# A planner's durations, a conversion cut into single steps and a broadcast matmul operand, in an attention and two-MLP kernel

## Chip, cores and metric

One NeuronCore of one Trainium2 chip runs the whole kernel in one launch. The metric is the device time of a run in microseconds. Engines are called as in the profile: PE is TensorE (PEld its weight loads), DVE is VectorE, ACT is ScalarE, POOL is GpSimd, SP is SyncE, whose queue issues every DMA of this kernel.

## What is computed

Inputs are q, k, v of 8 batches, 8 heads, 576 positions and 64 features, and five weight matrices. The weights come as float64 (the reference scales a float32 array with a numpy double), q, k, v as float32.

```python
q_s = softmax(q over the 64 features);  k_s = softmax(k over the 576 positions)
kv = einsum('bhsd,bhse->bhde', k_s, v);  x = einsum('bhsd,bhde->bhse', q_s, kv)   # 4608 x 512
h = x @ w_in;  x = relu(h)**2 @ w_out                      # w_in 512 x 2048
x = (sigmoid(x @ w_gate) * (x @ w_val)) @ w_out2           # w_gate, w_val 512 x 1536
```

## The kernel before, in words

**Work.** The 4608 tokens are cut into nine blocks `j` of 512; heads go in four pairs `p`. For each batch `b` and pair, `plan_k` (lines 604 to 621) loads keys and values and forms the 128x128 `kv`; for each block and pair, `plan_q` (623 to 659) makes the softmax of the queries and multiplies it with `kv` into `x`. [...] Blocks 0 to 2 go through the first MLP by plain products (`c_in`, `c_out`, lines 809 to 839); the other blocks, and all of the second MLP, go through units of seven products instead of eight (`plan_seven`, 768).

**Weights.** A raw weight block is 128x512 float64 (512 KB) in a buffer `wraw` of tag "W". Its conversion to float32 is done with integer operations: two on ACT (`w_abs` line 255, `w_low` line 261), then on DVE `w_bits`, which issues three instructions one behind the other on the same tile (a clip, line 268; a shift and mask, 269; the sign, 272), and `w_round` (line 279). Then the block is split (212, 215) and stored to a DRAM copy (`w_store`, line 297, or `w_store32`, line 310); later products fetch the copy (`w_fetch`, line 302). There are 68 raw blocks, 32 of them for the first MLP.

**Keys' maxima.** The maximum of each key feature over all positions is needed in all 128 partitions. `k_max` (411) takes maxima within a partition, `k_turn` (423) transposes on PE into PSUM, `k_diag` (428 to 434) reduces along the row to one value per partition, `m1` (line 431), and multiplies the identity matrix with it (line 433); `k_all` (436 to 438) multiplies a matrix of ones (stationary operand) with that diagonal (moving operand), which puts each maximum into all rows. `k_sub` (443) and `k_exp` (447) follow, then the product with the values (`k_mm`, 453) and its scaling (`k_rec` 457 and 458, `k_copy` 465).

**The order.** Nothing is left to a scheduler of the compiler: the class `Plan` (30 to 131) writes the order of every queue. Each step is added with a key (a due time, computed from constants such as T0 = 27.0 and TS0 = 4.4), the engines that it may use with its assumed duration in us, the steps it comes after, and the buffers it takes and gives. `Plan.trace` plays this list through: when an engine is idle in the plan, the ready step with the smallest key is issued to it, occupies it for the assumed duration, and its successors become ready after `LATENCY` more (2.0 us behind a DMA, 0.2 behind PE, 0.15 behind the others). A pair as a duration stands for "POOL idle, POOL busy"; no step is planned on POOL in this kernel, so the first value always counts (lines 103, 104). The plan's clock is used for the order alone. On the chip every queue runs in that order, and an instruction waits by semaphore for what it needs, with all that stands behind it in its queue. The assumed durations of the steps around the change are: DVE on a 128x512 tile 0.78 (`TT`, 199), `w_bits` 1.55, `w_round` 0.85, ACT on such a tile 0.60 to 0.66, `k_diag` 0.5, `k_mm` 1.3, a 512 KB DMA 1.5, a load of q 0.73. Steps of q and k of blocks above 4 are offered to PE 2.5 us late (`SLACK`, 601); those of blocks up to 4 are not.

Of the kernel before, what the change touches and what calls it, by code (L numbers as in the profile page):

```python
# [29 lines left out]
class Plan:  # L30
# [4 lines left out]
    LATENCY = {DMA: 2.0, PE: 0.2}  # L35
# [19 lines left out]
    def trace(self):  # L55
# [22 lines left out]
        while left:  # L78
            for e in ready:
                if busy[e] > now:  # L80
                    continue
                held = []
                short = set()
                while ready[e] and len(held) < self.LOOK:
                    key, n = heapq.heappop(ready[e])
                    if taken[n]:
                        continue
                    _, _, engines, name, fn, args, _, take, give, _ = self.ops[n]
                    if any(t in short for t in take) or any(self.free[t] < take.count(t) for t in take):
# [12 lines left out]
                    us = engines[e]  # L102
                    if isinstance(us, tuple):
                        us = us[busy[POOL] > now]
# [41 lines left out]
def attention_mlp_mlp(  # L146
# [44 lines left out]
    ones = cst.tile([128, 128], F32, name="ones")  # L191
# [7 lines left out]
    TT = (0.78, 1.1)  # L199
    VEC = {DVE: TT}  # L200
    LOW = {DVE: TT}
    ROUND = {DVE: 0.85}
# [208 lines left out]
    def k_max(b, p):  # L411
# [9 lines left out]
        kmx[b, p] = (a, mx[:, C:2 * C])  # L421

    def k_turn(b, p):
        ps = banks[p] if b == 0 else pa.tile([128, N], F32, tag="pa", name="kps")
        nc.tensor.transpose(ps[:, KT0:KT0 + 128], kmx[b, p][0], ident)
        kps[b, p] = ps

    def k_diag(b, p):
# [175 lines left out]
    def plan_k(b, p, key, step, wait=()):  # L604
# [5 lines left out]
        add(key, {DVE: (0.95, 1.9)}, ("kmx",) + n, k_max, b, p, after=[("kt",) + n], take=["km"])  # L610
        add(key + 0.5 * step, {PE: 0.3}, ("kt2",) + n, k_turn, b, p, after=[("kmx",) + n], take=bank, slack=slack(b))
        add(key + step, {DVE: (0.5, 0.85)}, ("kdg",) + n, k_diag, b, p, after=[("kt2",) + n])
        add(key + 1.5 * step, {PE: 0.4}, ("kgm",) + n, k_all, b, p, after=[("kdg",) + n], give=["km"], slack=slack(b))
        add(key + 2 * step, {DVE: 0.85}, ("ks",) + n, k_sub, b, p, after=[("kgm",) + n])
        add(key + 3 * step, {ACT: 0.75}, ("ke",) + n, k_exp, b, p, after=[("ks",) + n])
        add(key + 4 * step, {PE: 1.3}, ("kp",) + n, k_mm, b, p, after=[("ke",) + n, ("vt",) + n], give=big, slack=slack(b))
        add(key + 5 * step, {DVE: 0.4}, ("kr",) + n, k_rec, b, p, after=[("kp",) + n], take=["kr"])
# [5 lines left out]
    def plan_q(j, p, key, step, qmul):  # L623
# [3 lines left out]
        add(key, {DVE: 0.69}, ("qa",) + n, q_red, j, p, ALU.max, "qm", after=[("qt",) + n], take=["qm"])  # L627
# [4 lines left out]
        else:  # L632
            add(key + 0.5 * step, {DVE: (0.8, 0.9) if pe else (0.95, 1.2)}, ("qs",) + n, q_sub, j, p, after=[("qa" if pe else "qaw",) + n], give=["qm"] if pe else ["qm", "pa"])
        add(key + step, {ACT: 2.4 if j == JACT else 0.63}, ("qe",) + n, q_exp, j, p, after=[("qs",) + n], give=["qm"] if j == JACT else [])
        add(key + 2 * step, {DVE: 0.69}, ("qb",) + n, q_red, j, p, ALU.add, "qr", after=[("qe",) + n], take=["qr"])
        if not pe:
            add(key + 2.3 * step, {PE: 0.15}, ("qbw",) + n, q_swap, j, p, after=[("qb",) + n], take=["pa"], slack=slack(j))
        add(key + 2.5 * step, {DVE: (0.3, 0.6) if pe else (0.45, 0.9)}, ("qr",) + n, q_sum, j, p, after=[("qb" if pe else "qbw",) + n], give=[] if pe else ["pa"])
        if j == JACT:
            qmul = {ACT: 2.4}  # L640
# [127 lines left out]
    def plan_seven(uid, t, nb, n, pe, tags):  # L768
# [8 lines left out]
        ua = 0.6 if n > 256 else 0.35  # L777
        uv = 0.7 if n > 256 else 0.42
# [153 lines left out]
    def conv_in(j, f, t):  # L932
# [20 lines left out]
        add(t + 2.6, {ACT: 1.24}, ("cg", j, f), c_g, j, f, after=[("ch", j, f, KT - 1)], take=["f"])  # L953

    def conv_out(j, f, t):
# [7 lines left out]
        add(t - 2.5, {ACT: 0.62}, ("chi", j, f), c_hi, j, f, after=[("cg", j, f)], take=["S"])  # L963
# [91 lines left out]
    def in_stage(n, t):  # L1055
# [5 lines left out]
        for h in range(2):  # L1061
            G = ("G", n, h)
            gready = defaultdict(dict)
            for u in range(2):
# [12 lines left out]
            for kk in range(4):  # L1077
                for qn, (name, where) in gready[kk].items():
# [7 lines left out]
                    add(tk, {ACT: 0.63}, ("bhi", nm, qn), lambda nm=nm, qn=qn, bind=bind: (bind(), b_hi(nm, qn, qn, "S", nt)), after=[name], take=["S"])  # L1086
# [5 lines left out]
            for tq in range(2):  # L1092
# [16 lines left out]
                for oh in range(2):  # L1109
                    pr = use_pair[tq, oh]  # L1110
                    ends = []
                    for m in range(2):
# [7 lines left out]
                        add(t + 0.1, {DVE: 0.7} if h else {ACT: 0.6, DVE: 0.7}, nm, o_ev, key, pr[m], h, nt, CHOSEN, after=after, take=[] if h else ["a"])  # L1120
# [7 lines left out]
    def gate_stage(n, t):  # L1128
# [10 lines left out]
        for u in range(gv_n):  # L1139
# [5 lines left out]
            us = 0.62 if nt > 256 else 0.38  # L1145
            uv = 0.7 if nt > 256 else 0.42
# [83 lines left out]
    nc.gpsimd.memset(ones, 1.0)  # L1230
# [68 lines left out]
```

## Time and profile before

| what | value |
|---|---|
| median of 3 runs | 1712.14 us (1710.82 to 1718.0) |
| the profiled execution's own time | 1716.33 us |
| span of the profile (first to last instruction) | 1714.5 us |
| mean granted PE clock | 0.990 of full speed |
| instructions | 24259 |

The profile is of one execution. The span lies inside the execution's time; what lies around it is 1.8 us. A matmul's end in the trace is modelled, and matmuls overlap, so that a busy PE is one that always has a matmul in flight. In a timeline a line is: start, duration, engine, line of the kernel, operation, output and inputs, count, and in brackets how long the engine was idle before it and what ended that idle time.

### The profile page before, as it was taken

Reading aid. Unit: us, or ns where it says so; the run is one execution under the profiler, and the core shown is the slowest. Engines: PE = TensorE matmul, PEld = TensorE weight load, DVE = VectorE, ACT = ScalarE, POOL = GpSimd, SP = SyncE. Lnnn points to the kernel's source line nnn. Section 1 sums busy time; section 2 is a strip of 40 time slices with the busy share of each in tenths; the row PEclk is TensorE's granted clock in tenths of the full one; section 3 lists DMA queues with packets and bytes.
Section 4 is the critical chain, followed back from the end, with each engine's and each line's share of the span. In section 5 each row is a group of like instructions: output and inputs, shape, how many; then the busy total and the mean of one; then the engine's idle time right before and its main releaser. Section 6 shows DMA issues by size and latency. Waiting matters only on the chain.

```text
span 1714.5 us, 24259 instructions
## 1 busy us (share of the span) xinstructions
PE 1666.9 (97%) x8788; PEld 1425.3 (83%) x8788; DVE 1127.2 (66%) x2109; ACT 916.4 (53%) x1649; POOL 2.1 (0%) x15
## 2 busy tenths in 40 slices
PE   5889999999999999999999999999999999999999
PEld 3668878787788788878898889988888899889999
DVE  7978746788888665775785757741624485448556
ACT  4986544557576565653554655552723454335344
POOL 0000000000000000000000000000000000000000
PEclk8989999999999999999999999999999999999999
DMA  6999878799787889799757555755576557655797
GB/s 228 335 329 325 312 241 289 250 324 368 255 309 267 321 293 349 270 370 335 246 185 243 190 188 172 237 201 183 186 249 194 195 190 246 204 196 178 245 378 270
DMA packets 149144, 443.23 MB, mean 259 GB/s; under 512 B 15648, under 2 KB 24864, under 8 KB 149024
## 3 DMA queue, kind: packets, MB, share of 16 engines
q1 hardware_dynamic: 149024, 441.68, 74.1%
q8 instruction: 70, 1.15, 0.3%
q14 instruction: 50, 0.41, 0.1%
HBM read 354.06 MB, written 87.56 MB: 258 GB/s over the span
## 4 chain that ended last, share of the span: by engine, by line
PE 85%; DMA 7%; DVE 4%; ACT 2%; issue 1%; SPq 1%; ACTq 0%; DVEq 0%
PE bank L218 27%; PE bank L220 27%; PE bank L219 27%; PE xps L580 2%; PE kps L453 1%; DMA qt<-in_q_dram 1%; DMA ws<-w_in 1%; DMA wraw<-in_moe_w_gate_dram 1%; DMA wraw<-in_moe_w_out_dram 1%; DMA vt<-in_v_dram 1%; DMA ws<-w_gv 1%; DVE whl L215 0%; PE qsw L511 0%; PE bank L453 0%; ACT wf L255 0%
## 5 line engine op out<-in xcount | busy, mean ns | idle before, releaser
L218 PE MATMUL bank<-bX,ws 128*128 128x512 f32 (+1 forms) x1176 | 446.3, 379 | 7.2 <-DMA ws<-w_in 5.7
L220 PE MATMUL bank<-bX,ws 128*128 128x512 f32 (+1 forms) x1176 | 440.7, 375 | 0.0
L219 PE MATMUL bank<-bX,ws 128*128 128x512 f32 (+1 forms) x1176 | 440.7, 375 | 0.0
L739 DVE TENSOR_TENSOR s<-s,bank 128x512 f32<-128x512 f32 (+1 forms) x279 | 179.9, 651 | 215.4 <-PE bank L220 178.4
L212 ACT ACTIVATE s<-bank 128x512 f32<-128x512 f32 (+1 forms) x279 | 156.7, 568 | 215.4 <-PE bank L220 213.7
L218 PEld LDWEIGHTS bank<-bX,ws 128*128 128x128 f32 x1176 | 222.0, 189 | 47.5 <-DMA ws<-w_in 4.7
L220 PEld LDWEIGHTS bank<-bX,ws 128*128 128x128 f32 x1176 | 221.7, 189 | 40.3
L219 PEld LDWEIGHTS bank<-bX,ws 128*128 128x128 f32 x1176 | 222.1, 189 | 37.7 <-issue 0.5
L212 ACT ACTIVATE bS<-s 128x512 fp32r<-128x512 f32 (+1 forms) x282 | 166.1, 597 | 147.1 <-PE bank L220 129.7
L215 DVE TENSOR_TENSOR bS<-s,bS 128x512 fp32r<-128x512 f32 (+1 forms) x282 | 180.9, 650 | 75.2 <-ACT bS L212 67.7
L218 PE MATMUL bank<-ws,bS 128*128 128x256 f32 x756 | 214.6, 284 | 0.0
L220 PE MATMUL bank<-ws,bS 128*128 128x256 f32 x756 | 213.9, 283 | 0.0
L219 PE MATMUL bank<-ws,bS 128*128 128x256 f32 x756 | 213.9, 283 | 0.0
L218 PE MATMUL bank<-bS,ws 128*128 128x512 f32 x384 | 150.5, 392 | 0.0
L220 PE MATMUL bank<-bS,ws 128*128 128x512 f32 x384 | 149.5, 389 | 0.0
L219 PE MATMUL bank<-bS,ws 128*128 128x512 f32 x384 | 149.5, 389 | 0.0
L218 PEld LDWEIGHTS bank<-ws,bS 128*128 128x128 f32 x756 | 145.0, 192 | 1.0 <-issue 0.2
L219 PEld LDWEIGHTS bank<-ws,bS 128*128 128x128 f32 x756 | 145.0, 192 | 0.9 <-issue 0.2
L220 PEld LDWEIGHTS bank<-ws,bS 128*128 128x128 f32 x756 | 145.0, 192 | 0.0
L758 ACT ACTIVATE s<-s 128x512 f32<-128x512 f32 (+1 forms) x120 | 70.4, 588 | 136.4 <-DVE s L739 136.2
L212 ACT ACTIVATE whl<-wf 128x512 fp32r<-128x512 f32 x111 | 68.0, 624 | 42.2 <-PE bank L220 12.0
L215 DVE TENSOR_TENSOR whl<-wf,whl 128x512 fp32r<-128x512 f32 x111 | 74.1, 685 | 20.3 <-ACT whl L212 19.3
(122 smaller groups left out, 2419.8 us busy)
## 6 DMA issues: line engine op xcount, KB each, us to landing
ws<-w_gv SPq DMA_DIRECT2D x210, 512.0 KB, 4.3
ws<-w_out SPq DMA_DIRECT2D x185, 512.0 KB, 4.3
ws<-w_in SPq DMA_DIRECT2D x116, 512.0 KB, 6.0
w_gv<-whl SPq DMA_DIRECT2D x42, 512.0 KB, 5.7
w_out<-whl SPq DMA_DIRECT2D x37, 512.0 KB, 6.2
w_in<-whl SPq DMA_DIRECT2D x32, 512.0 KB, 4.4
wraw<-in_moe_w_out_dram SPq DMA_DIRECT2D x28, 512.0 KB, 6.1
vt<-in_v_dram SPq DMA_DIRECT2D x32, 325.0 KB, 5.9
```

The lines of the kernel that those rows point to most:

```text
L212: nc.scalar.activation(out=dst, in_=src, func=AF.Copy)
L215: by_name[engine].tensor_tensor(out=dst, in0=src, in1=hi.bitcast(F32), op=ALU.subtract)
L218: nc.tensor.matmul(ps, ah, bh, start=first, stop=False, skip_group_check=True)
L219: nc.tensor.matmul(ps, ah, bl, start=False, stop=False, skip_group_check=True)
L220: nc.tensor.matmul(ps, al, bh, start=False, stop=last, skip_group_check=True)
L453: nc.tensor.matmul(ps[:, 0:2 * D + 1], kt[:, r, :], vt[:, r, 0:2 * D + 1], start=(r == 0), stop=(r == RK - 1))
L580: nc.tensor.matmul(ps[:, e], kvf[b % 2][p], t[:, e], start=True, stop=True)
L739: nc.vector.tensor_tensor(out=t, in0=t, in1=banks[pr[b]][:, 0:n], op=ALU.add)
L758: nc.scalar.activation(out=t, in_=t, func=AF.Sigmoid)
```

## The change

Three edits.

1. **Keys' maxima.** `k_diag` loses the multiplication with the identity and becomes `k_col`; `k_all` takes `m1`, a 128x1 tile, as stationary operand read 128 times (`to_broadcast`), and the identity as the moving one. The tile of ones and its memset go.
2. **Conversion.** `w_bits` is planned as three steps, `w_clip`, `w_bits` and `w_sign`, of one instruction each, with keys 0.05 apart. The instructions are the same.
3. **The planner's durations.** Pairs are gone; almost every duration on DVE and ACT, and some on PE, are other numbers, and `LATENCY` gets entries for DVE and ACT. Durations of DMAs, the due times, the buffers and `SLACK` stay.

The diff, cut to its core:

```diff
-    LATENCY = {DMA: 2.0, PE: 0.2}
+    LATENCY = {DMA: 2.0, PE: 0.2, DVE: 0.13, ACT: 0.15}
...
-    TT = (0.78, 1.1)
+    TT = 0.61
...
-    ROUND = {DVE: 0.85}
+    ROUND = {DVE: TT}
+    AS, AP = 0.53, 0.5
...
+    def w_clip(key):
+        t = wf[key]
+        nc.vector.tensor_scalar(out=t, in0=t, scalar1=E_MIN, scalar2=E_MAX, op0=ALU.max, op1=ALU.min)
+
     def w_bits(key):
-        _, high = w_words(key)
         t = wf[key]
         w = t.bitcast(I32)
-        nc.vector.tensor_scalar(out=t, in0=t, scalar1=E_MIN, scalar2=E_MAX, op0=ALU.max, op1=ALU.min)
         nc.vector.tensor_scalar(
             out=w, in0=w, scalar1=3, scalar2=0x3FFFFFF8, op0=ALU.logical_shift_left, op1=ALU.bitwise_and
         )
+
+    def w_sign(key):
+        _, high = w_words(key)
+        w = wf[key].bitcast(I32)
         nc.vector.scalar_tensor_tensor(
             out=w, in0=high, scalar=-0x40000000, in1=w, op0=ALU.bitwise_and, op1=ALU.bitwise_or
         )
...
-        add(t, {ACT: 0.63}, ("wh",) + key, w_hi, key, b, htag, after=after, take=[htag])
+        add(t, {ACT: AS}, ("wh",) + key, w_hi, key, b, htag, after=after, take=[htag])
...
-            add(t, {ACT: 0.66}, ("wa",) + key, w_abs, key, tag, after=[("wl",) + key])
-            add(t + 0.1, {ACT: 0.66}, ("wc",) + key, w_low, key, after=[("wl",) + key])
-            add(t + 0.2, {DVE: (1.55, 2.05)}, ("wb",) + key, w_bits, key, after=[("wa",) + key])
-            add(t + 0.4, ROUND, ("wr",) + key, w_round, key, CHOSEN, after=[("wb",) + key, ("wc",) + key], give=["W"])
+            add(t, {ACT: 0.57}, ("wa",) + key, w_abs, key, tag, after=[("wl",) + key])
+            add(t + 0.1, {ACT: 0.57}, ("wc",) + key, w_low, key, after=[("wl",) + key])
+            add(t + 0.2, {DVE: 0.35}, ("wp",) + key, w_clip, key, after=[("wa",) + key])
+            add(t + 0.25, {DVE: 0.35}, ("wb",) + key, w_bits, key, after=[("wp",) + key])
+            add(t + 0.3, {DVE: TT}, ("wg",) + key, w_sign, key, after=[("wb",) + key])
+            add(t + 0.4, ROUND, ("wr",) + key, w_round, key, CHOSEN, after=[("wg",) + key, ("wc",) + key], give=["W"])
...
-    def k_diag(b, p):
+    def k_col(b, p):
         m1 = sp.tile([128, 1], F32, tag="km1", name="km1")
         nc.vector.tensor_reduce(out=m1, in_=kps[b, p][:, KT0:KT0 + 128], axis=AX.X, op=ALU.max)
-        _, dg = kmx.pop((b, p))
-        nc.vector.tensor_scalar(out=dg, in0=ident, scalar1=m1, scalar2=None, op0=ALU.mult)
-        kmx[b, p] = dg
+        kmx[b, p] = m1
 
     def k_all(b, p):
-        nc.tensor.matmul(kps[b, p][:, KM0:KM0 + 2 * D], ones, kmx.pop((b, p)), start=True, stop=True)
+        m1 = kmx.pop((b, p)).to_broadcast([128, 128])
+        nc.tensor.matmul(kps[b, p][:, KM0:KM0 + 2 * D], m1, ident, start=True, stop=True)
...
-        add(key + step, {DVE: (0.5, 0.85)}, ("kdg",) + n, k_diag, b, p, after=[("kt2",) + n])
+        add(key + step, {DVE: 0.22}, ("kdg",) + n, k_col, b, p, after=[("kt2",) + n])
...
-        add(key + 4 * step, {PE: 1.3}, ("kp",) + n, k_mm, b, p, after=[("ke",) + n, ("vt",) + n], give=big, slack=slack(b))
+        add(key + 4 * step, {PE: 1.15}, ("kp",) + n, k_mm, b, p, after=[("ke",) + n, ("vt",) + n], give=big, slack=slack(b))
...
-        add(key + step, {ACT: 2.4 if j == JACT else 0.63}, ("qe",) + n, q_exp, j, p, after=[("qs",) + n], give=["qm"] if j == JACT else [])
+        add(key + step, {ACT: 2.1 if j == JACT else AS}, ("qe",) + n, q_exp, j, p, after=[("qs",) + n], give=["qm"] if j == JACT else [])
...
-        ua = 0.6 if n > 256 else 0.35
-        uv = 0.7 if n > 256 else 0.42
+        ua = AP if n > 256 else 0.28
+        uv = TT if n > 256 else 0.34
...
```

The lines that are left out put `AS` (0.53) for 0.62 to 0.63 and `AP` (0.5) for 0.6 on ACT, `TT` (0.61) for 0.69 to 0.85 on DVE, 1.12 for 1.24 in the two-instruction steps on ACT, and small cuts of the same kind elsewhere.

## Rows read from the trace of the kernel before

**Rows 1.** The page: busy us of each engine, share of the span, instructions.
```profile
PE 1666.9 (97%) x8788; PEld 1425.3 (83%) x8788; DVE 1127.2 (66%) x2109; ACT 916.4 (53%) x1649; POOL 2.1 (0%) x15
```

**Rows 2.** Busy time by stretch: stretch, length, PE, PEld, DVE, ACT, POOL, clock, DMA share, GB/s.
```profile
0.00:20.00 20.00, 8.58 (x38) 6.53 (x39) 13.89 (x38) 8.67 (x16) 2.10 (x15) 1.00 0.82 297
20.00:40.00 20.00, 12.58 (x41) 8.13 (x40) 15.93 (x37) 10.96 (x21) 0.00 (x0) 0.64 0.38 144
40.00:120.00 80.00, 69.20 (x300) 51.82 (x299) 66.48 (x147) 69.53 (x165) 0.00 (x0) 0.92 0.94 333
120.00:860.00 740.00, 725.78 (x3352) 600.19 (x3352) 542.13 (x1036) 431.88 (x763) 0.00 (x0) 1.00 0.84 301
860.00:1715.00 855.00, 850.76 (x5064) 758.62 (x5062) 488.73 (x854) 395.34 (x687) 0.00 (x0) 1.00 0.65 216
```

**Rows 3.** DVE's timeline from 20 to 45 us.
```profile
22.45 0.42 DVE L268 TENSOR_SCALAR wf<-wf 128x512 f32<-128x512 f32 x1
22.90 0.43 DVE L269 TENSOR_SCALAR wf<-wf 128x512 int32<-128x512 int32 x1
23.36 0.69 DVE L272 SCALAR_TENSOR_TENSOR wf<-wraw,wf 128x512 int32<-128x512 int32 x1
24.95 0.16 DVE L457 TENSOR_SCALAR kri<-bank 128x1 f32<-128x1 f32 x1 [0.90 <-PE bank L453]
...
26.27 0.29 DVE L431 TENSOR_REDUCE km<-bank 128x1 f32<-128x128 f32 x1 [0.38 <-PE bank L425]
26.60 0.29 DVE L433 TENSOR_SCALAR kmx<-ident,km 128x128 f32<-128x128 f32 x1
...
32.72 0.69 DVE L215 TENSOR_TENSOR x<-xps,x 128x512 fp32r<-128x512 f32 x1 [0.91 <-ACT x L212]
34.24 0.16 DVE L457 TENSOR_SCALAR kri<-bank 128x1 f32<-128x1 f32 x1 [0.83 <-PE bank L453]
...
34.82 0.64 DVE L279 CUSTOM_DVE_ANT_0 wf<-wraw,wf 128x1024 uint16<-128x1024 uint16 x1
35.37 0.69 DVE L557 TENSOR_TENSOR qt<-qt,qst 128x512 f32<-128x512 f32 x1
35.97 0.69 DVE L279 CUSTOM_DVE_ANT_0 wf<-wraw,wf 128x1024 uint16<-128x1024 uint16 x1
```

**Rows 4.** The SP queue's timeline, the two issues between 23 and 36 us.
```profile
29.29 0.33 SPq L489 DMA_DIRECT2D qt<-in_q_dram  x1
35.48 0.33 SPq L310 DMA_DIRECT2D w_in<-wf  x1
```

**Rows 5.** The chain of waits in order of time: one values product early, one later.
```profile
22.40 2.52 PE bank L453 x10
...
226.27 1.11 PE kps L453 x10
```

**Rows 6.** PE's waits from 120 us on: line, releaser, us in total, times, longest.
```profile
PE bank L218 <- DMA ws<-w_in: 5.7, 4, 2.9
PE qsw L511 <- DVE qst L501: 3.0, 2, 1.9
PE bank L218 <- DMA ws<-w_gv: 1.5, 1, 1.5
```

**Rows 7.** Groups by line and form: busy us and mean ns of one, idle time before.
```profile
L438 PEld LDWEIGHTS kps<-kmx,ones 128*128 128x128 f32 x56 | 10.1, 188 | 3.8 <-DVE kmx L433 2.0
L511 PEld LDWEIGHTS qsw<-qst,swap 128*128 128x128 f32 x112 | 19.3, 189 | 12.8 <-DVE qst L501 3.8 <-DVE x L215 2.8 <-ACT xf L212 1.5
L433 DVE TENSOR_SCALAR kmx<-ident,km 128x128 f32<-128x128 f32 x32 | 9.2, 287 | 1.1
L535 ACT ACT_TABLE_LOAD x9 | 11.5, 1283 | 5.5 <-DMA qt<-in_q_dram 4.4 <-DVE qt L526 1.0
```

**Rows 8.** DMA issues: kind, count, KB each, median us from issue to landing.
```profile
ws<-w_in SPq DMA_DIRECT2D x116, 512.0 KB, 6.0
...
qt<-in_q_dram SPq DMA_DIRECT2D x36, 256.0 KB, 4.5
```

More of the change, by code (lines that the diff above doesn't have):

```diff
@@ L102, in trace @@
                     us = engines[e]
-                    if isinstance(us, tuple):
-                        us = us[busy[POOL] > now]
                     busy[e] = now + us
@@ L190, in attention_mlp_mlp @@
     ident = cst.tile([128, 128], F32, name="ident")
-    ones = cst.tile([128, 128], F32, name="ones")
     swap = cst.tile([128, 128], F32, name="swap")
@@ L420, in k_max @@
             nc.vector.tensor_tensor(out=a, in0=a, in1=kt[:, r * C:r * C + C], op=ALU.max)
-        kmx[b, p] = (a, mx[:, C:2 * C])
+        kmx[b, p] = a
     def k_turn(b, p):
         ps = banks[p] if b == 0 else pa.tile([128, N], F32, tag="pa", name="kps")
-        nc.tensor.transpose(ps[:, KT0:KT0 + 128], kmx[b, p][0], ident)
+        nc.tensor.transpose(ps[:, KT0:KT0 + 128], kmx[b, p], ident)
         kps[b, p] = ps
-    def k_diag(b, p):
+    def k_col(b, p):
         m1 = sp.tile([128, 1], F32, tag="km1", name="km1")
         nc.vector.tensor_reduce(out=m1, in_=kps[b, p][:, KT0:KT0 + 128], axis=AX.X, op=ALU.max)
-        _, dg = kmx.pop((b, p))
-        nc.vector.tensor_scalar(out=dg, in0=ident, scalar1=m1, scalar2=None, op0=ALU.mult)
-        kmx[b, p] = dg
+        kmx[b, p] = m1
     def k_all(b, p):
-        nc.tensor.matmul(kps[b, p][:, KM0:KM0 + 2 * D], ones, kmx.pop((b, p)), start=True, stop=True)
+        m1 = kmx.pop((b, p)).to_broadcast([128, 128])
+        nc.tensor.matmul(kps[b, p][:, KM0:KM0 + 2 * D], m1, ident, start=True, stop=True)
     def k_sub(b, p):
@@ L609, in plan_k @@
         add(key - 4 if b else p + 4, {DMA: 0.92}, ("vt",) + n, v_load, b, p, after=wait, take=big[1:])
-        add(key, {DVE: (0.95, 1.9)}, ("kmx",) + n, k_max, b, p, after=[("kt",) + n], take=["km"])
-        add(key + 0.5 * step, {PE: 0.3}, ("kt2",) + n, k_turn, b, p, after=[("kmx",) + n], take=bank, slack=slack(b))
-        add(key + step, {DVE: (0.5, 0.85)}, ("kdg",) + n, k_diag, b, p, after=[("kt2",) + n])
-        add(key + 1.5 * step, {PE: 0.4}, ("kgm",) + n, k_all, b, p, after=[("kdg",) + n], give=["km"], slack=slack(b))
-        add(key + 2 * step, {DVE: 0.85}, ("ks",) + n, k_sub, b, p, after=[("kgm",) + n])
-        add(key + 3 * step, {ACT: 0.75}, ("ke",) + n, k_exp, b, p, after=[("ks",) + n])
-        add(key + 4 * step, {PE: 1.3}, ("kp",) + n, k_mm, b, p, after=[("ke",) + n, ("vt",) + n], give=big, slack=slack(b))
-        add(key + 5 * step, {DVE: 0.4}, ("kr",) + n, k_rec, b, p, after=[("kp",) + n], take=["kr"])
+        add(key, {DVE: 0.95}, ("kmx",) + n, k_max, b, p, after=[("kt",) + n], take=["km"])
+        add(key + 0.5 * step, {PE: 0.12}, ("kt2",) + n, k_turn, b, p, after=[("kmx",) + n], take=bank, slack=slack(b))
+        add(key + step, {DVE: 0.22}, ("kdg",) + n, k_col, b, p, after=[("kt2",) + n])
+        add(key + 1.5 * step, {PE: 0.25}, ("kgm",) + n, k_all, b, p, after=[("kdg",) + n], give=["km"], slack=slack(b))
+        add(key + 2 * step, {DVE: 0.74}, ("ks",) + n, k_sub, b, p, after=[("kgm",) + n])
+        add(key + 3 * step, {ACT: AS}, ("ke",) + n, k_exp, b, p, after=[("ks",) + n])
+        add(key + 4 * step, {PE: 1.15}, ("kp",) + n, k_mm, b, p, after=[("ke",) + n, ("vt",) + n], give=big, slack=slack(b))
+        add(key + 5 * step, {DVE: 0.35}, ("kr",) + n, k_rec, b, p, after=[("kp",) + n], take=["kr"])
         add(
@@ L626, in plan_q @@
         add(key - 5 if j else p + 0.1, {DMA: 0.73}, ("qt",) + n, q_load, j, p, after=x_before.get(j, []), take=["q"])
-        add(key, {DVE: 0.69}, ("qa",) + n, q_red, j, p, ALU.max, "qm", after=[("qt",) + n], take=["qm"])
+        add(key, {DVE: 0.61}, ("qa",) + n, q_red, j, p, ALU.max, "qm", after=[("qt",) + n], take=["qm"])
         if not pe:
@@ L632, in plan_q @@
         else:
-            add(key + 0.5 * step, {DVE: (0.8, 0.9) if pe else (0.95, 1.2)}, ("qs",) + n, q_sub, j, p, after=[("qa" if pe else "qaw",) + n], give=["qm"] if pe else ["qm", "pa"])
-        add(key + step, {ACT: 2.4 if j == JACT else 0.63}, ("qe",) + n, q_exp, j, p, after=[("qs",) + n], give=["qm"] if j == JACT else [])
-        add(key + 2 * step, {DVE: 0.69}, ("qb",) + n, q_red, j, p, ALU.add, "qr", after=[("qe",) + n], take=["qr"])
+            add(key + 0.5 * step, {DVE: TT if pe else 0.78}, ("qs",) + n, q_sub, j, p, after=[("qa" if pe else "qaw",) + n], give=["qm"] if pe else ["qm", "pa"])
+        add(key + step, {ACT: 2.1 if j == JACT else AS}, ("qe",) + n, q_exp, j, p, after=[("qs",) + n], give=["qm"] if j == JACT else [])
+        add(key + 2 * step, {DVE: 0.61}, ("qb",) + n, q_red, j, p, ALU.add, "qr", after=[("qe",) + n], take=["qr"])
         if not pe:
             add(key + 2.3 * step, {PE: 0.15}, ("qbw",) + n, q_swap, j, p, after=[("qb",) + n], take=["pa"], slack=slack(j))
-        add(key + 2.5 * step, {DVE: (0.3, 0.6) if pe else (0.45, 0.9)}, ("qr",) + n, q_sum, j, p, after=[("qb" if pe else "qbw",) + n], give=[] if pe else ["pa"])
+        add(key + 2.5 * step, {DVE: 0.36 if pe else 0.55}, ("qr",) + n, q_sum, j, p, after=[("qb" if pe else "qbw",) + n], give=[] if pe else ["pa"])
         if j == JACT:
-            qmul = {ACT: 2.4}
+            qmul = {ACT: 2.1}
         add(key + 3 * step, qmul, ("qm",) + n, q_mul, j, p, CHOSEN, after=[("qr",) + n], give=["qr"])
@@ L644, in plan_q @@
         else:
-            add(key + 4 * step, {DVE: 0.72}, ("qT",) + n, q_turn, j, p, after=[("qm",) + n], take=["a"], give=["q"])
+            add(key + 4 * step, {DVE: 0.63}, ("qT",) + n, q_turn, j, p, after=[("qm",) + n], take=["a"], give=["q"])
         if pe:
-            add(key + 5 * step, {ACT: 0.6}, ("qh",) + n, q_copy, j, p, after=[("qT",) + n], take=["a"], give=["pa"])
+            add(key + 5 * step, {ACT: AP}, ("qh",) + n, q_copy, j, p, after=[("qT",) + n], take=["a"], give=["pa"])
         bs = [b for _, b in segs(j)]
         add(
-            key + 7 * step, {PE: 1.0}, ("xp",) + n, q_mm, j, p, after=[("qh" if pe else "qT",) + n] + [("kv", b, p) for b in bs],
+            key + 7 * step, {PE: 0.92}, ("xp",) + n, q_mm, j, p, after=[("qh" if pe else "qT",) + n] + [("kv", b, p) for b in bs],
             take=["pa"], give=["a"], slack=slack(j),
@@ L655, in plan_q @@
         if j < NONE:
-            add(key + 8 * step, {ACT: 0.6}, ("xh",) + n, x_hi, j, p, after=[("xp",) + n], take=[XTAG[j]])
-            add(key + 9 * step, {DVE: 0.7}, ("x",) + n, x_lo, j, p, after=[("xh",) + n], give=["pa"])
+            add(key + 8 * step, {ACT: AP}, ("xh",) + n, x_hi, j, p, after=[("xp",) + n], take=[XTAG[j]])
+            add(key + 9 * step, {DVE: TT}, ("x",) + n, x_lo, j, p, after=[("xh",) + n], give=["pa"])
             return
-        add(key + 8 * step, {ACT: 0.6}, ("x",) + n, x_copy, j, p, after=[("xp",) + n], take=["x"], give=["pa"])
+        add(key + 8 * step, {ACT: AP}, ("x",) + n, x_copy, j, p, after=[("xp",) + n], take=["x"], give=["pa"])
     bq = {}
@@ L679, in plan_b @@
     def plan_b(nm, ready, times, tag, n, gives):
-        us = 0.63 if n > 256 else 0.38
-        ub = VEC if n > 256 else {DVE: (0.43, 0.6)}
+        us = AS if n > 256 else 0.32
+        ub = VEC if n > 256 else {DVE: 0.34}
         lo = lambda i: ("blo", nm, i)
@@ L952, in conv_in @@
                 add(t, {FREE: 0.0}, ("cf", j, f, kt), lambda: None, after=[("ch", j, f, kt)] + ([] if j else [("ws", "in", g, i)]), give=[tag])
-        add(t + 2.6, {ACT: 1.24}, ("cg", j, f), c_g, j, f, after=[("ch", j, f, KT - 1)], take=["f"])
+        add(t + 2.6, {ACT: 1.12}, ("cg", j, f), c_g, j, f, after=[("ch", j, f, KT - 1)], take=["f"])
     def conv_out(j, f, t):
@@ L962, in conv_out @@
             conv_fetch(j, "out", g, ii, t)
-        add(t - 2.5, {ACT: 0.62}, ("chi", j, f), c_hi, j, f, after=[("cg", j, f)], take=["S"])
+        add(t - 2.5, {ACT: AS}, ("chi", j, f), c_hi, j, f, after=[("cg", j, f)], take=["S"])
         add(t - 2, LOW, ("clo", j, f), c_lo, j, f, CHOSEN, after=[("chi", j, f)], give=["f"])
@@ L973, in conv_out @@
             for o in range(KT):
-                add(t + 3, {ACT: 0.6} if o % 2 == 0 else {DVE: 0.7}, ("cev", j, o), c_ev, o, after=[("co", j, f)], take=["a"])
+                add(t + 3, {ACT: AP} if o % 2 == 0 else {DVE: TT}, ("cev", j, o), c_ev, o, after=[("co", j, f)], take=["a"])
                 add(t + 4, {DMA: 0.8}, ("ost", j, o, 1), c_st, j, o, after=[("cev", j, o)], give=["a"])
@@ L1070, in in_stage @@
                     for nm in ("s1", "s5", "s2"):
-                        add(t - 1, {ACT: 1.24, DVE: TT}, E(nm + "g", b), e_relu2, uid, nm, b, CHOSEN, after=[end[nm][b]])
-                    add(t + 0.2, {ACT: 1.24}, E("p4g", b), e_relu2p, uid, "p4", prs[0], b, nt, "f", after=[end["p4"][b]], take=["f"])
+                        add(t - 1, {ACT: 1.12, DVE: TT}, E(nm + "g", b), e_relu2, uid, nm, b, CHOSEN, after=[end[nm][b]])
+                    add(t + 0.2, {ACT: 1.12}, E("p4g", b), e_relu2p, uid, "p4", prs[0], b, nt, "f", after=[end["p4"][b]], take=["f"])
                     fin.append(E("p4g", b))
@@ L1085, in in_stage @@
                     tk = t + (4 * tq + kk) * 24 * mm * SLOW - 6
-                    add(tk, {ACT: 0.63}, ("bhi", nm, qn), lambda nm=nm, qn=qn, bind=bind: (bind(), b_hi(nm, qn, qn, "S", nt)), after=[name], take=["S"])
+                    add(tk, {ACT: AS}, ("bhi", nm, qn), lambda nm=nm, qn=qn, bind=bind: (bind(), b_hi(nm, qn, qn, "S", nt)), after=[name], take=["S"])
                     add(tk + 0.1, LOW, ("blo", nm, qn), b_lo, nm, qn, qn, CHOSEN, after=[("bhi", nm, qn)], give=["f"])
@@ L1119, in in_stage @@
                             after.append(("old",) + key)
-                        add(t + 0.1, {DVE: 0.7} if h else {ACT: 0.6, DVE: 0.7}, nm, o_ev, key, pr[m], h, nt, CHOSEN, after=after, take=[] if h else ["a"])
+                        add(t + 0.1, {DVE: TT} if h else {ACT: AP, DVE: TT}, nm, o_ev, key, pr[m], h, nt, CHOSEN, after=after, take=[] if h else ["a"])
                         add(t + 1, {DMA: 0.8}, ("ost",) + key[:2] + (h,) + key[2:], o_st, key, h, c, after=[nm], give=["a"])
@@ L1144, in gate_stage @@
             fin = []
-            us = 0.62 if nt > 256 else 0.38
-            uv = 0.7 if nt > 256 else 0.42
+            us = AS if nt > 256 else 0.32
+            uv = TT if nt > 256 else 0.34
             for b in range(2):
@@ L1194, in gate_stage @@
             nm = ("e", uid, "p4", b)
-            add(t, {ACT: 0.6, DVE: 0.7}, nm, z_copy, uid, prs[0], b, N, "a", CHOSEN, after=[end["p4"][b]], take=["a"])
+            add(t, {ACT: AP, DVE: TT}, nm, z_copy, uid, prs[0], b, N, "a", CHOSEN, after=[end["p4"][b]], take=["a"])
             fin.append(nm)
@@ L1229, in attention_mlp_mlp @@
     make_identity(nc, ident)
-    nc.gpsimd.memset(ones, 1.0)
     halves = [x.rearrange("p (a b c) -> p a b c", b=2, c=32) for x in (swap, ident)]
```

## The prediction

> **What bounds the kernel now.** I read the busy times first: PE is in use for 1666.9 of 1714.5 us [rows 1]. So 47.6 us without a matmul in flight are what better order can win back, and besides them what PE lost at its lower clock: 0.990 granted on the mean is 1.0% of 1714.5, at most 17 us. Next, busy times by stretch, to see where these lie [rows 2]. PE is idle for 11.4 us of the first 20, 7.4 of the next 20, 10.8 from 40 to 120, 14.2 from 120 to 860, and 3.7 after that, which is the tail behind the last product. From 860 us on PE never waits: nothing that DVE, ACT or an order does there can shorten anything.
>
> Then each stretch's own limit. From 40 to 120 us the DMA engines are busy for 0.94, beside ACT at 69.5 and DVE at 66.5 of 80 us; from 20 to 40 us they are busy for only 0.38, while PE runs at a granted 0.64 (1.0 is 2.4 GHz and 0.5 is 1.2 GHz) [rows 2]. A queue that is soon to be short of DMA time wastes it there. DVE's timeline shows why [rows 3]: the sign step of the first converted weight block starts at 23.36, its rounding step, which needs nothing else of DVE, only at 34.82. Between them DVE stands four times, for 0.90, 0.38, 0.91 and 0.83 us, before a step that needs PE or ACT, with the rounding step behind it in its queue. SP stands too: behind its issue at 29.29 (0.33 long) it issues nothing until 35.48, the store of that block [rows 4]. From 120 us on, PE's waits [rows 6] are half DMA (5.7 and 1.5 of 14.2 us); the rest end on ACT or DVE steps of keys and queries.
>
> **Why the order is as it is.** The plan before takes a 512-wide DVE step for 0.78 us and the keys' product for 1.3, so 1.7 DVE steps fit beside one product. On the chip DVE steps follow each other at 0.60 (35.37 to 35.97) [rows 3], and the product takes 2.52 us at the start and 1.11 later [rows 5]: 4.2 steps fit beside it early, 1.9 later. The new plan has 1.15 over 0.61, so 1.9. A load of q is planned at 0.73 + 2.0 = 2.73 us, 3.5 old or 4.5 new DVE steps; its median is 4.5 us, 7.5 real ones [rows 8]. So the old plan lets DVE reach the steps that wait for PE or DMA too soon; the new one errs the same way, but less.
>
> **The change, part by part.**
>
> Keys' maxima. The multiplication with the identity goes: 32 instructions, 9.2 us of DVE [rows 7]. On a chain it costs 0.33 us (26.27 to 26.60) [rows 3]; only the four chains of the first batch run while PE has nothing else, so between 0 and 4 x 0.33 = 1.3 us; I take 1.0. Everywhere else PE's other products hide it. The product itself keeps shape and type, so no gain is possible there. Its stationary operand is now one element read 128 times, a load that the trace doesn't show. The nearest rows, loads from the tile of ones and from the swap matrix, cost 188 and 189 ns, whatever they load [rows 7]; I take no cost. Were each of the 64 loads (two for each of 32 products) to take twice its time, it would be 64 x 0.19 = 12 us on PE. The memset of ones was POOL's and lies beside the first load of keys: nothing.
>
> Conversion as single steps. Two dependent steps start 0.45 and 0.46 us after each other for durations of 0.42 and 0.43, so each costs its duration and 0.03. Independent ones start 0.55 and 0.60 apart for 0.64 and 0.69, so their duration less 0.09 [rows 3]. Another step behind each of three saves 3 x 0.12 = 0.36 us per block, 24 us of DVE over 68 blocks, but DVE is idle a third of the span. What counts is the first four blocks: at most 1.4 us; half of it, 0.7, since the plan won't always have another step ready. The other end is +1.8: three strangers of 0.6 us inside the one block that PE waits for. The Trainium skill (VectorE: DVE Perf Modes, "The DRAIN you can't avoid") says that the next operation doesn't start until the pipe is empty, and that leaving out semaphores gains nothing. By that this term would be 0 and the sum 0.7 us smaller. The trace speaks against it: independent steps do start before the one ahead has ended.
>
> Durations, first 40 us. If the rounding steps move up into DVE's four gaps (3.0 us together, room for five steps) the first store could go out up to 34.82 - 24.95 = 9.9 us sooner, and the raw loads behind it on SP with it. The first MLP product needs x of four head pairs too, whose PE work keeps its place, so not all of it reaches the end. Bounds 0 and -10; I take the middle, -5.
>
> Durations, 40 to 120 us. PE idles 10.8 us, but DMA at 0.94 has 0.06 x 80 = 4.8 us to give. Bounds -4.8 and +3 (the same again of one bad wait); I take -2.
>
> Durations, 120 to 860 us. The DMA half of PE's waits stays: no DMA's duration changes, and fetches still stand on SP behind stores that wait for DVE. Of the other 7.0 us I take 2 off. Bounds -7 and +14 (all waits doubled). After 860 us: nothing, PE covers it.
>
> **Sum.** -1.0 - 0.7 - 5 - 2 - 2 = -10.7 us. The profiled execution took 1716.33 us (1714.5 of span and 1.8 around it), 4.2 above the median of the runs, so it would become 1705.6; against the median 1712.14 it is 1701.4. I forecast 1701.
>
> **Rivals.**
>
> *Nothing to measure.* The due times are the same, and durations decide only where several steps are ready. The DMA-bound stretch ends when it did, and only the first two terms are left: 1712.1 - 1.7 = 1710. For it: 0.94 DMA share after 40 us, PE never idle after 860. Against: the 0.38 before.
>
> *Slower: PE's queue between 120 and 860 us.* The old durations were a cushion: a DVE step planned at 0.78 ran at 0.60, so PE's small products for queries and keys (lines 511, 425, 438) stood late enough in PE's queue. With 0.61 there is none, yet a q load lands 1.8 us after its planned time (4.5 against 2.73) [rows 8] and ACT's table loads, 1.28 us each [rows 7], are in no plan. Then PE stands at such a product with all weight products behind it. Blocks 2 to 4 have no added slack: 12 query chains. At 1.5 us each, as in the two such waits of the trace [rows 6], nine or ten of them make the +14 of the bound above. If the start wins nothing beyond 1.7 us, the time is 1724. It decides once PE's idle time in this stretch goes from 14.2 over 14.2 + 1.7 + 8.6 = 24.5 us. Against it: PE waited for ACT or DVE only seven us in 740.
>
> *All ends good:* the low bounds together are -24.5, 1688.
>
> *The repeated operand is slow:* 12 us of PE on top of the forecast, 1713.
>
> **How the numbers follow.** Half a per cent, 8.6 us, is about what can be told from no change: below 1703.6 is faster, above 1720.7 slower. Chances: forecast 0.46 (its own range 1693 to 1708), nothing to measure 0.25, slower 0.14, all good 0.12, slow operand 0.03. The forecast's lower two thirds, the all-good case and a little of the second are faster: 0.47. Slower is the PE queue and a little of the bounds (+14, +3): 0.15. The rest, 0.38, is within. The range runs from the all-good case, 1687, to near the slow rival, 1721; outside it lie the slow rival's own time and what is beyond the good bounds.
>
> **What would show it.** Right: the first rounding step well before 34.8 us, SP's gap at 29 to 35 us gone, the DMA share of 20 to 40 us over 0.5 and PE idle below 16 us before 40 us; no instruction of line 433's kind; weight loads of the keys' product still at 0.19 us; conversion steps with other DVE steps between them; PE's idle time in 120 to 860 us at 10 to 14 us. Wrong: PE idle above 24 us there (the cushion), or a first 40 us that look the same. The forecast is also wrong if PE waits after 860 us, where I expect none.

## The result and the profile after

The change made the kernel slower: 1726.11 us median of 5 runs (1723.38 to 1730.83) against 1710.82 before (1709.88 to 1718.0), a ratio of 1.0083 [1.0064, 1.0102]. The profiled execution is the fastest of its five, 1723.38 us, and that of before (1716.33) lies above its median, so the two spans differ by 7.1 us only, where the medians differ by 15.3: what follows splits the 7.1. The page of the changed kernel, busy times:

```profile
span 1721.6 us, 24185 instructions
...
PE 1668.4 (97%) x8788; PEld 1423.5 (83%) x8788; DVE 1104.4 (64%) x2076; ACT 915.4 (53%) x1652; POOL 1.9 (0%) x14
```

Its busy time by stretch, columns as in [rows 2]; the last line is cut out of the one above it:

```profile
0.00:20.00 20.00, 9.78 (x41) 7.47 (x42) 14.34 (x38) 9.76 (x17) 1.95 (x14) 1.00 0.79 283
20.00:40.00 20.00, 15.26 (x61) 10.61 (x60) 17.54 (x42) 11.94 (x24) 0.00 (x0) 0.83 0.68 249
40.00:120.00 80.00, 73.30 (x328) 54.75 (x327) 71.09 (x162) 77.45 (x181) 0.00 (x0) 0.96 0.98 343
120.00:860.00 740.00, 712.63 (x3250) 585.53 (x3250) 515.38 (x984) 418.91 (x742) 0.00 (x0) 0.99 0.84 296
...
340.00:360.00 20.00, 9.29 (x34) 7.17 (x33) 19.86 (x38) 9.70 (x17) 0.00 (x0) 0.74 0.81 301
```

PE's idle time is the stretch less its busy time. In the first 120 us it fell from 29.6 to 21.7 us, and from 20 to 40 us the granted clock rose from 0.64 to 0.83 and the DMA share from 0.38 to 0.68 [rows 2]. From 120 to 860 us it rose from 14.2 to 27.4. So -8.0 and +13.2, a tail 0.4 longer and 1.5 of PE's own busy time make the 7 us. The early gain is real and is lost behind it, with more.

PE's waits from 120 us on (line, releaser, us in total, times, longest), against [rows 6]:

```profile
PE kps L431 <- DVE kmx L426: 9.1, 1, 9.1
PE qsw L516 <- ACT xf L210: 5.1, 3, 2.2
PE bank L216 <- ACT s L210: 4.3, 2, 3.0
PE bank L216 <- ACT xo L210: 1.7, 1, 1.7
PE qsw L516 <- DVE qst L524: 1.5, 1, 1.5
PE qsw L516 <- ACT kv L470: 1.5, 1, 1.5
...
PE kps L443 <- DVE km L437: 0.9, 1, 0.9
```

No DMA is named any more: PE waits for ACT and DVE, and two thirds of the time (some 18 of 27.4 us) at the small products of keys and queries, lines 431, 443 and 516 (425, 438 and 511 of before). The largest wait ends at 353.60, in a stretch where DVE hardly idles (19.86 of 20 us busy), and PE's clock is down to 1.2 GHz behind it (0.50 granted from 353.6 to 358 us, 0.74 over the stretch). ACT's waits from 120 to 860 us show what ACT itself stands behind:

```profile
ACT wf L253 <- DMA wraw<-in_moe_w_val_dram: 29.3, 8, 8.0
...
ACT wf L253 <- DMA wraw<-in_moe_w_out_dram: 28.5, 11, 7.4
...
ACT wf L253 <- DMA wraw<-in_moe_w_gate_dram: 15.5, 7, 3.5
```

73 us before conversions whose raw block has not landed. Before had the same wait, for 54 us:

```profile
ACT wf L255 <- DMA wraw<-in_moe_w_out_dram: 30.5, 16, 5.8
...
ACT wf L255 <- DMA wraw<-in_moe_w_gate_dram: 13.3, 5, 4.4
...
ACT wf L255 <- DMA wraw<-in_moe_w_val_dram: 10.6, 4, 5.1
```

Another wait shows in the timelines of ACT and DVE some 40 us ahead of PE's long one, where a block is split into its rounded part (ACT, L210) and the rest (DVE, L213):

```profile
305.71 0.63 ACT L210 ACTIVATE whl<-wf 128x512 fp32r<-128x512 f32 x1 [3.84 <-DMA w_in<-whl]
```
```profile
301.91 0.69 DVE L213 TENSOR_TENSOR whl<-wf,whl 128x512 fp32r<-128x512 f32 x1 [0.77 <-ACT whl L210]
306.38 0.69 DVE L213 TENSOR_TENSOR whl<-wf,whl 128x512 fp32r<-128x512 f32 x1 [3.78 <-ACT whl L210]
```

ACT wants to write a buffer whose store has not landed; DVE waits for ACT. That these few us reach PE's long wait is not shown. The plan gives a store's buffer back 1.5 us after its issue and takes a load as landed after 1.5 + 2.0 us; the DMA issues (KB each, median us to landing) of this kernel say otherwise:

```profile
ws<-w_out SPq DMA_DIRECT2D x185, 512.0 KB, 4.3
...
w_in<-whl SPq DMA_DIRECT2D x32, 512.0 KB, 4.4
...
wraw<-in_moe_w_out_dram SPq DMA_DIRECT2D x28, 512.0 KB, 6.2
```

So 512 KB take 4.3 to 6.2 us here, as medians over the whole run. The Trainium skill (DMA: Bandwidth & Descriptors, "Anatomy of one DMA") gives about 2.0 us as the fixed cost of a DMA beside the moving of its data, the planner's figure, but for DMAs on GpSimd's path; SP issues all of this kernel's, so no run here shows that figure.

### The profile page after: what moved, and what is told of

The parts are those of the page before. It is cut to its first block, busy times and chain, and to the rows that moved or that the text cites. A ratio compares the mean times of both kernels' runs of the same rounds, so it can differ in the third digit from the quotient of the medians.

```text
span 1721.6 us, 24185 instructions
## 1 busy us (share of the span) xinstructions
PE 1668.4 (97%) x8788; PEld 1423.5 (83%) x8788; DVE 1104.4 (64%) x2076; ACT 915.4 (53%) x1652; POOL 1.9 (0%) x14
## 4 chain that ended last, share of the span: by engine, by line
PE 81%; DMA 7%; DVE 5%; ACT 4%; issue 1%; SPq 1%; ACTq 0%; DVEq 0%
PE bank L216 26%; PE bank L218 26%; PE bank L217 26%; DMA w_gv<-whl 2%; DMA wraw<-in_moe_w_gate_dram 2%; PE xps L585 1%; DMA wraw<-in_moe_w_out_dram 1%; PE kps L458 1%; DMA qt<-in_q_dram 1%; DVE whl L213 1%; ACT whl L210 1%; DVE wf L276 1%; DVE wf L283 1%; ACT wf L253 1%; DVE qst L506 0%
## 5 line engine op out<-in xcount | busy, mean ns | idle before, releaser
L210 ACT ACTIVATE s<-bank 128x512 f32<-128x512 f32 (+1 forms) x279 | 156.0, 568 | 196.8 <-PE bank L218 196.2
L210 ACT ACTIVATE bS<-s 128x512 fp32r<-128x512 f32 (+1 forms) x282 | 165.5, 596 | 136.2 <-PE bank L218 120.8
L213 DVE TENSOR_TENSOR bS<-s,bS 128x512 fp32r<-128x512 f32 (+1 forms) x282 | 180.0, 646 | 65.3 <-ACT bS L210 64.2
L210 ACT ACTIVATE whl<-wf 128x512 fp32r<-128x512 f32 x111 | 68.6, 626 | 60.2 <-DVE wf L283 22.1
L213 DVE TENSOR_TENSOR whl<-wf,whl 128x512 fp32r<-128x512 f32 x111 | 75.1, 685 | 23.4 <-ACT whl L210 23.0
```

Source lines behind the costliest of these rows:

```text
L210: nc.scalar.activation(out=dst, in_=src, func=AF.Copy)
L213: by_name[engine].tensor_tensor(out=dst, in0=src, in1=hi.bitcast(F32), op=ALU.subtract)
```

## The experiments

Four theories. **No cushion**: the old durations above the chip's pace gave DVE slack (my slower rival). **Planned hole**: the new order has one fault of its own, PE's wait near 350 us. **Late DMAs**: the plan takes every DMA for too short, and how much that costs depends on the order by chance. **The instructions**: the edits themselves cost. All results first. Before was run again beside each group of runs, and the ratio is to those runs. Idle is PE's, from the one profile of each kernel, by stretch: e1, in the order of before, has 18.9 where before has 14.2, so a difference of 5 us between two rows tells little. The last column is what the planner takes behind a DMA, and when its buffers come back.

| run | ratio to before, 95% | idle 0-120 | idle 120-860 | DMA in the plan |
|---|---|---|---|---|
| before | 1 | 29.6 | 14.2 | 2.0, early |
| the change | 1.0083 [1.0064, 1.0102] | 21.7 | 27.4 | 2.0, early |
| e1 keys only | 1.0000 [0.9983, 1.0016] | 29.6 | 18.9 | 2.0, early |
| e2 durations only | 1.0094 [1.0066, 1.0121] | 25.1 | 27.1 | 2.0, early |
| e3 change, 0.78 on DVE | 1.0110 [1.0084, 1.0137] | 23.7 | 33.8 | 2.0, early |
| e5 change, mended line | 1.0044 [1.0028, 1.0060] | 24.9 | 20.9 | 2.0, early |
| e6 change, 0.60 for 0.61 | 1.0088 [1.0052, 1.0125] | 22.8 | 31.0 | 2.0, early |
| e11 before, mended line | 1.0089 [1.0064, 1.0113] | 30.1 | 24.9 | 2.0, early |
| e12 before, 0.77 for 0.78 | 1.0101 [1.0075, 1.0127] | 28.0 | 22.8 | 2.0, early |
| e13 before, 0.70 for 0.78 | 1.0115 [1.0090, 1.0140] | 33.2 | 22.6 | 2.0, early |
| e8 change, mended line | 0.9967 [0.9950, 0.9983] | 24.2 | 12.9 | 3.5, early |
| e4 change | 0.9932 [0.9912, 0.9952] | 22.8 | 14.1 | 3.5, at landing |
| e7 change, mended line | 0.9842 [0.9809, 0.9876] | 23.1 | 1.9 | 3.5, at landing |
| e9 before, mended line | 0.9886 [0.9871, 0.9901] | 27.8 | 4.4 | 3.5, at landing |
| e10 e7, durations only | 0.9889 [0.9871, 0.9906] | 28.7 | 3.6 | 3.5, at landing |
| e14 e7, no single steps | 0.9917 [0.9899, 0.9936] | 25.7 | 5.3 | 3.5, at landing |

**e1, the keys' edit alone**, in the order of before.

```diff
-        nc.tensor.matmul(..., ones, kmx.pop((b, p)), ...)
+        nc.tensor.matmul(..., kmx.pop((b, p)).to_broadcast([128, 128]), ident, ...)
```

> The kernel before with the keys' edit alone (maxima as broadcast stationary operand, no multiplication with the identity); every planned duration and so the order of every queue stays as before. Theory 'no cushion' (the new durations let the plan run ahead of what loads and stores deliver, DVE has no slack to catch up, and PE waits in 120 to 860 us): like before or up to 1.3 us faster, PE idle in 120 to 860 us near 14 us. Rival 'the instructions cost' (the repeated operand is a slow weight load, or the conversion's steps are drawn out): 6 to 15 us slower, weight loads of the keys' product above 0.3 us. Rival 'luck of the order' (any other order moves PE's waits about by chance): order unchanged, so as before.

No difference. The weight loads in the changed kernel, by form (busy us, mean ns), beside the 188 ns of [rows 7]:

```profile
L443 PEld LDWEIGHTS kps<-ident,km 128*128 128x128 f32 x56 | 9.9, 188 | 4.4 <-DVE km L437 2.9
```

One element per partition, read 128 times, loads as fast as a tile. "The instructions" falls for this edit.

**e2, the new durations alone.**

```diff
-            add(t + 0.2, {DVE: 0.35}, ("wp",) + key, w_clip, ...)      # and the two steps behind it
+            add(t + 0.2, {DVE: 1.55}, ("wg",) + key, lambda key: (w_clip(key), w_bits(key), w_sign(key)), ...)
```

> The changed kernel with the keys' edit taken back (ones and diagonal again, planned at 0.42) and the conversion planned as one step of 1.55 again: the new durations alone. 'No cushion': slower than before by 8 to 18 us, like the whole change; PE idle in 120 to 860 us 22 us or more, in 0 to 120 us under 25. 'The instructions cost': like before, within 4 us. 'Luck of the order': anywhere from 12 us below to 20 above before.

As slow as the whole change: the loss comes with the new order, not with what the two edits issue.

**e3, DVE's cushion given back.**

```diff
-    TT = 0.61
+    TT = 0.78
```

> The changed kernel with the one constant for a 512-wide DVE step planned at 0.78 as before, all else new. 'No cushion': DVE has its slack back, so PE idle in 120 to 860 us falls to 16 us or less, and what the first 120 us won is kept at least in part: 2 to 14 us faster than before. 'The instructions cost': slower than before by 10 to 16 us, like the change. 'Luck of the order': no telling, PE idle in 120 to 860 us between 10 and 30 us.

Slower still, 33.8 us idle. This speaks against "no cushion", though other durations differ from before too, and 12.4 of the 33.8 us are one wait at line 431, the hole taken up below; without it 21.4 are left, still over the 16 expected.

**e4, DMAs as late as they are.**

```diff
-    LATENCY = {DMA: 2.0, ...
+    LATENCY = {DMA: 3.5, ...
-                    heapq.heappush(events, (now + us, 0, n))
+                    heapq.heappush(events, (now + us + (self.LATENCY[DMA] if e == DMA else 0.0), 0, n))
```

> The changed kernel with all its new durations, but the planner takes 3.5 us instead of 2.0 behind each DMA before its successors are ready, and gives a DMA's buffers back only then instead of at the end of its 1.5 or 0.8 us (the median landing is 4.3 to 6.0 us after issue). 'No cushion', with late DMAs as its root: PE idle in 120 to 860 us falls from 27 to under 18 us, and the kernel is 2 to 14 us faster than before. If the cushion of DVE alone matters, whatever makes it late: still 20 us or more idle there, and slower than before. 'The instructions cost': 10 to 16 us slower than before. 'Luck of the order': no telling.

Faster than before, with all the new durations. Of 14.1 us idle one wait is 10.7: PE's waits from 120 to 860 us.

```profile
PE kps L431 <- DVE kmx L426: 10.7, 1, 10.7
PE qsw L516 <- DVE qst L524: 1.8, 2, 1.0
```

**e5, e6, the hole.** The same wait at the same step stands in the change (9.1 us), e2 (9.7), e3 (12.4) and e4 (10.7), so it is in the plan. SP's timeline in the changed kernel shows the order: after 340.95 (the issue at 340.05 takes 0.90) SP issues nothing for 6.8 us, then a store that waited for DVE, one raw load, and only then the fetches that the next products need.

```profile
340.05 0.90 SPq L494 DMA_DIRECT2D qt<-in_q_dram  x2
347.71 0.33 SPq L301 DMA_DIRECT2D w_gv<-whl  x1
348.13 0.38 SPq L243 DMA_DIRECT2D wraw<-in_moe_w_val_dram  x1
348.56 2.39 SPq L306 DMA_DIRECT2D ws<-w_out  x4
```

In the code, a step that lacks a buffer puts every kind it would take on the list `short` (line 90 of before), and later steps may take none of these. A raw load takes a "W" and a "w"; while it lacks a "w" it keeps the fetches from free "W" buffers. Played through by itself, without the chip, the planner of the changed kernel leaves PE idle for 11.2 us of the plan's clock ahead of this step; in e5 and e6 it leaves no gap over 2.4 us from 120 to 860.

```diff
-                        short.update(take)
+                        short.update(t for t in take if t in short or self.free[t] < take.count(t))
```

> The changed kernel with one line of the planner mended: a step that lacks one kind of buffer no longer keeps later steps from the other kinds that it would take, of which some are free. Theory 'planned hole' (in the changed order a raw weight load that lacks a 'w' buffer is planned ahead of the fetches of the first MLP's second matrix, which need only a 'W' buffer; they are issued behind it, and PE stands 9 us near 344 us, cold behind it): that wait of 9 to 12 us is gone, granted clock from 340 to 360 us back over 0.9, time 10 to 16 us below the change, 1709 to 1717 or within 5 us of before; PE idle in 120 to 860 us 14 to 20 us, all of it short waits. Rival 'late DMAs' alone (the hole is only lag of DVE): the wait of 9 us stays or shows up elsewhere, and it is as slow as the change.

e6 is the change with `TT = 0.60`.

> The changed kernel with one constant 2% lower, 0.60 for 0.61, by which the planner happens to issue these fetches ahead of that raw load. 'Planned hole': as in the run with the mended line, 10 to 16 us below the change, no wait of PE over 4 us between 300 and 400 us. 'Late DMAs' alone: a cushion smaller still, so as slow as the change or slower.

The hole goes in both, no wait is longer than 3.7 us, and the granted clock from 340 to 360 us is back at 1.00. e5 won 0.4%, less than the 10 to 16 us expected, and e6 nothing: shorter waits fill its place. The hole is real but alone isn't the loss.

**e7, e8, both, and landings without buffers.** e7 is e4 with the mended line; e8 keeps 3.5 us but gives buffers back early.

> Both together: the mended line, and DMAs that take 3.5 us behind their issue and hold their buffers until then (the run before with late DMAs took 0.993 of before and still had the hole, 10.7 us). 'Planned hole' and 'late DMAs' as two separate losses: the hole goes and short waits stay few, so 10 to 15 us below that run, 1686 to 1694, 0.984 to 0.989 of before. If late DMAs had mattered only by chance of the order: 1700 to 1715.

> The mended line, and 3.5 us behind each DMA before its successors are ready, but its buffers given back early, as in the change. If what the plan gets wrong is above all when loads land: as good as with both, 1686 to 1696. If it is that a stored buffer is reused too early in the plan (ACT held for 3.8 us by a store near 302 us in the change): PE idle in 120 to 860 us over 12 us, 1700 to 1714.

e7: 1687.36 us, faster than both kernels. PE's only wait from 120 to 860 us, and ACT's waits for raw blocks there (13.7 us where the change had 73 and before 54):

```profile
PE bank L216 <- DMA ws<-w_in: 1.9, 1, 1.9
```
```profile
ACT wf L253 <- DMA wraw<-in_moe_w_val_dram: 7.7, 3, 6.0
...
ACT wf L253 <- DMA wraw<-in_moe_w_out_dram: 5.4, 4, 2.1
...
ACT wf L253 <- DMA wraw<-in_moe_w_gate_dram: 0.6, 1, 0.6
```

The mended line is worth 0.9% here (e4 to e7), though in the kernel before, at 2.0 us, it costs as much (e11 below). The later landing alone is worth 0.8% (e5 to e8), and giving the buffers back only then another 1.3% (e8 to e7): the second of e8's two forecasts, with 12.9 us idle.

**e9, e10, e14, what the durations and edits are worth in such a plan.** e9 is before, e10 and e14 the change with both or one edit taken back, all with e7's two edits to the planner.

> The kernel before, all its own durations, with the two edits of the run that took 0.984: the mended reservation line, and DMAs that take 3.5 us behind their issue and hold their buffers until then. Theory 'right paces pay only in a plan that is right about DMAs too': without the new paces it stays 8 us or more above that run, 0.989 to 1.002 of before. Rival 'the old durations were merely a stand-in for late DMAs, and the new ones are worth nothing in themselves': 0.980 to 0.987, like that run.

> The run that took 0.984 with the keys' edit and the single steps of the conversion taken back: new durations, mended line and late DMAs alone. If the two small edits are worth what I forecast for them (1.7 us): 0.984 to 0.988. If the single steps matter more in an order that holds (DVE spends 0.36 us less on each of 68 blocks and other steps get between): 0.989 to 0.995.

> The run that took 0.984 (mended line, late DMAs, all of the change) with the conversion planned as one step of 1.55 again; the keys' edit stays. With both edits taken back it was 0.989. If the single steps make the difference: 0.988 to 0.991, PE idle in the first 120 us near 29 us as there. If the keys' edit does: 0.983 to 0.986, near 23 us.

Old and new durations give the same, 0.9886 and 0.9889: by themselves they are worth nothing, against what e9's first theory said. With the single steps 0.9917 becomes 0.9842; the keys' edit gives nothing in time (e10, e14). e14's other sign is mixed: 25.7 us idle in the first 120 lies between the 29 and the 23 that it was to choose from.

**e11, e12, e13, is before a good draw?** The mended line, then 0.77, then 0.70 for 0.78, in the kernel before.

> The kernel before with the mended line alone. The order before has no wait of PE over 3 us after 20 us, so 'planned hole' expects little: 0.994 to 1.002. If the line costs something everywhere: 0.985 to 0.992.

> The kernel before with one planned duration 1% lower, 0.77 for 0.78 on a 512-wide DVE step; DMAs stay as before. Theory 'before is a lucky draw' (in a plan that is wrong about DMAs nearly any other order costs 0.5 to 1.1%; before's is one of the better ones): 1.004 to 1.012 of before, PE idle in 120 to 860 us over 20 us. Rival 'a cushion' (what saved the kernel before are DVE durations well above the chip's 0.60): 1% less of it changes nothing, 0.997 to 1.003.

> The same with 0.70 for 0.78. 'Lucky draw': again 1.004 to 1.012, no slower than with 0.77. 'A cushion': half of it is gone, so clearly slower than with 0.77, 1.004 to 1.008 where that one is 1.000.

One per cent of one assumed duration costs as much as the whole change, and so does the mended line, which I had expected to do nothing. A cushion hardly shrinks by 1%, and with half of it gone (e13) the kernel is not clearly slower than that: that theory falls. In e12 PE waits longest for DMAs:

```profile
PE bank L218 <- DMA ws<-w_in: 7.8, 2, 7.0
PE bank L218 <- DMA ws<-w_gv: 3.2, 1, 3.2
```

Of the nine orders made with DMAs at 2.0 us (e1 has before's), before's is the fastest and the other eight are 0.4 to 1.2% slower; all five made with late landings and held buffers are 0.7 to 1.6% faster.

## Why the prediction was wrong

**What bounds it.** Right: PE never waits after 860 us but for the tail, and the early DMA share was a loss to be won back.

**Keys' maxima.** Forecast -1.0 and no cost of the load. Right on the load, 188 ns; the -1.0 is less than e1 can tell from nothing (its interval is 0.17% either way, about 3 us).

**Single steps.** I took -0.7, at most -1.4, because DVE is idle a third of the time. In the change itself the term can't be told (e2 and the change: intervals overlap). In e7's plan it reads as 0.75% (e14 to e7, 11 to 13 us), far over the bound; PE's idle time falls by 2.6 us in the first 120 and by 3.4 behind, from one profile each. If that is the steps' doing, the term was mis-sized. But cutting a step in three also makes another order, and whether a small change in another number moves this plan as far was not tried. How other steps can run between two dependent ones is seen in DVE's timeline of the changed kernel, where two clips of two blocks take 0.76 us together:

```profile
24.98 0.76 DVE L263 TENSOR_SCALAR wf<-wf 128x512 f32<-128x512 f32 x2
...
31.42 1.29 DVE L283 CUSTOM_DVE_ANT_0 wf<-wraw,wf 128x1024 uint16<-128x1024 uint16 x2
```

0.76 less the 0.42 of one is 0.34 from start to start, where the dependent steps of [rows 3] have 0.45. The section of the Trainium skill that the prediction sets against this (VectorE: DVE Perf Modes, "The DRAIN you can't avoid") also says that a next operation starts earlier if it is not held back, so it does not make the term 0, and these early starts do not contradict it.

**Durations, first 120 us.** Right in size: -5 and -2 stand against -3.9 us of idle time up to 40 us and -4.1 from there to 120, part of it the edits'. The way there held in part. The first rounding step went from 34.82 to 31.42 and its store from 35.48 to 32.17, but SP's gap is not gone: it now stands from 24.23 to 31.74 before a load of q, most of it for DVE.

```profile
23.90 0.33 SPq L494 DMA_DIRECT2D qt<-in_q_dram  x1
31.74 0.33 SPq L494 DMA_DIRECT2D qt<-in_q_dram  x1
32.17 0.89 SPq L314 DMA_DIRECT2D w_in<-wf  x2
```

The durations alone gave 4.5 us of the gain (e2), and with late DMAs hardly any (27.8 in e9, 28.7 in e10).

**Durations, 120 to 860 us.** The step that failed. I wrote that the DMA half of PE's waits stays, because no DMA's duration changes, and took 2 us off the rest. It was +13.2, near the bound of +14, and neither half did as forecast: the 7.2 us that ended on a DMA are gone, and the rest went from 7.0 to 27.4. That a DMA keeps its duration says nothing on when its successors stand in their queues. What the runs showed instead: one wait of 9.1 us is a hole of the plan's own, and the others come with a plan that has every DMA land too soon and so places steps ahead of their data. With late DMAs the same durations and edits leave 14.1 us, 10.7 of them the hole (e4), and with the mended line too 1.9 us (e7). Each new order made with 2.0 us places such steps elsewhere, and eight of eight came out slower. I had the row (4.5 against 2.73 us [rows 8]) and used it for an engine's pace and in the slower rival, not as the planner's larger fault.

**The rivals.** *Slower* had nearly the time (1724) and the place, PE's small products for keys and queries, with 0.14 too little chance; its sign, over 24.5 us idle, came with 27.4. Its mechanism, DVE's lost cushion, did not hold (e12, e13; and e9 against e10). *Slow operand* did not occur, nor *nothing to measure*.

**Open.** Why before's order is the good one was not tried; that it lies at the good end is shown, no more. Nor was it tried which loads or stores matter most, a landing time other than 3.5 us, or how far the time of e7 moves when one of its numbers does.

## What to carry to other kernels

When a planner writes the order, correct its worst number first: with a wrong landing time of DMAs each new set of durations was a gamble, and when it was mended, the better durations by themselves were worth nothing. Before reading a loss or a gain of under a per cent into an edit that reorders everything, move one assumed number by 1% and see how far the time goes. A planner may be starved by its own bookkeeping: look at what an idle queue is kept from, not only at what it waits for.

## What the runs showed of the hardware

A stationary operand read from one element per partition costs PE no more than a full tile, 188 ns a load. And one profile is one draw: the same order with 32 instructions fewer (e1, profiled at 1721.29 us) stands for 18.9 us from 120 to 860 us where before (1716.33) stands for 14.2, with the same median time over 10 and 13 runs.
